# Decode attention beside a Mish block: keys loaded in 32 KB runs, scores made piece by piece, three value buffers for four

## The chip, the cores and the metric

One core of a Trainium2 chip runs the whole program. The time is the device time of one execution in microseconds; a kernel's time is the median over its runs. The profile shows one further execution instruction by instruction.

## The reference

One decode step of a transformer layer whose attention branch and dense branch stand side by side:

```python
xn = layernorm(x)                                   # x: 2 x 1 x 448
q = (xn @ wq) as 16 heads of 256                    # 8 key/value heads, 2 query heads on each
k, v = the last 4096 of 32768 cached rows per head  # 2 x 8 x 4096 x 256
p = softmax(q k^T / 16)
attn = (p v, heads joined) @ wo                     # 4096 x 448
h = xn @ w1 + b1                                    # 448 x 1792
dense = (h * tanh(softplus(h))) @ w2                # 1792 x 448
out = x + attn + dense
```

All inputs are bfloat16. The windows of the two caches are 33.55 MB each; the four weight matrices bring the traffic to 77.66 MB. There is one token per sequence, so each cached number is used for two query heads only.

## The kernel before, in words

**Units.** The 16 (batch, head) streams are worked on in U = 4 units of J = 4 streams. A unit has 8.39 MB of keys and 8.39 MB of values. Four key tiles (`load_k(u, r)`, r = 0 to 3) and four value tiles (`load_v(u, g)`, g = 0 to 3) of 2.097 MB bring them: 128 partitions of 16 KB, each a contiguous run in the cache. For keys, a partition is one of 32 chunks of 128 rows of one stream, so that its four tiles are four consecutive quarters of 64 KB. For values, a partition has 32 consecutive rows.

**Keys.** VectorE transposes each key tile in 32 x 32 blocks (`turn`, L267) into two buffers `kt[0]` and `kt[1]`: each of them holds one half of the rows of all four tiles, so a scores call needs the first or the second half of every tile of the unit. `scores(u, i)` (L329) adds a mask with one matmul, then makes the scores with 32 matmuls on four column groups of TensorE; ScalarE takes the exponential (L351), and VectorE transposes it to the probabilities `p_t[i]` (L357). `weigh(u)` sums them.

**Values.** `values(u, g)` (L389) multiplies with 16 matmuls into one PSUM tile. `gather` copies that tile and folds it, `finish` divides by the sum, `relay` and `mix_early` apply the output projection of a unit as soon as its weight `wo` is there. `carry` moves what they have gathered to the accumulator of the last unit, whose last value tile has a form of its own (`values_fixed`) and whose projection (`mix`) is followed by the down projection of the dense branch (`dense_out`), in the order of the four pieces in which its weight arrives (`load_w2`).

**Order.** The schedule is written out by hand: each engine runs its instructions in the order in which the program has them. All large loads stand in SyncE's queue. A load into a buffer whose earlier contents are still being read waits in that queue, and what stands behind it waits too. Buffers per partition: three key tiles of 16 KB (`k_pool`), and a ring of four value tiles of 16 KB (`v_pool`) that also takes the query projection's weight in two pieces and the up projection's.

In each unit the loads stand in the order: four values of this unit, three keys of the next, the output weight, the fourth key. The scores of a unit come after all four of its key tiles have been transposed, and before its values.

Of the kernel before, what the change touches and what calls it, by code (L numbers as in the profile page):

```python
# [17 lines left out]
def kernel(  # L18
# [13 lines left out]
    nc = tc.nc  # L32
    P = 128
    G = 4
    J = 4
    R = 4

    Bsz, Sq, D = A_x.shape
    _, Hkv, Sk, Dh = A_k_cache.shape
# [24 lines left out]

    ctx.enter_context(tc.manual_schedule())

    k_pool = ctx.enter_context(tc.tile_pool(name="kk", bufs=3))
    v_pool = ctx.enter_context(tc.tile_pool(name="vv", bufs=4))
    kt_pool = ctx.enter_context(tc.tile_pool(name="kt", bufs=1))
    wo_pool = ctx.enter_context(tc.tile_pool(name="wo", bufs=2))  # L70
    p_pool = ctx.enter_context(tc.tile_pool(name="pp", bufs=1))
# [17 lines left out]
    k_t, v_t, wo_t = {}, {}, {}  # L89

    def load_k(u, r):
        t = k_pool.tile([P, KE], BF16, tag="k", name="k")
        src = kview[u][:, s0:, :].rearrange("j (c t) d -> c j (t d)", c=C)
        nc.sync.dma_start(out=t[:], in_=src[:, :, r * KE : (r + 1) * KE])  # L94
        k_t[u, r] = t

    def load_v(u, g, lo=0, hi=T):
        if lo == 0:
            v_t[u, g] = ring("v")
        t = v_t[u, g]  # L100
        src = vview[u][:, s0:, :].rearrange("j (g x t) d -> g x j (t d)", g=G, x=C)
        nc.sync.dma_start(
            out=t[:, lo * Dh : hi * Dh], in_=src[g, :, :, lo * Dh : hi * Dh]
        )

    def load_wo(u):
        w = wo_pool.tile([P, KU, rep, 2 * D], BF16, tag="wo", name="wo")
        if u < U - 1:
            nc.sync.dma_start(
                out=w[:].rearrange("p k h e -> p (k h e)"),  # L110
                in_=A_wo.rearrange("(k u y i) d -> u y k (i d)", k=KU, u=U, i=8)[u],
            )
        for k2 in range(KU if u == U - 1 else 0):
            r0 = (u + U * k2) * rep * Dh
            nc.sync.dma_start(  # L115
                out=w[:, k2, :, :],
                in_=A_wo[r0 : r0 + rep * Dh, :].rearrange("(h p c) d -> p h (c d)", h=rep, p=P),
            )
        wo_t[u] = w
# [4 lines left out]
    nc.scalar.dma_start(out=b1_sb[:], in_=B_b1.rearrange("(k q c) -> q k c", k=2, q=P))  # L124

    load_k(0, 0)
    load_k(0, 1)
    wq_t = []
    wq_in = A_wq.flatten().rearrange("(p e) -> p e", p=P)
    for lo, hi in ((0, 4), (4, NS)):  # L130
        t = ring("wq")
        nc.sync.dma_start(out=t[:, 0 : (hi - lo) * HW], in_=wq_in[:, lo * HW : hi * HW])
        wq_t += [t[:, i * HW : (i + 1) * HW] for i in range(hi - lo)]
    load_k(0, 2)

    ident = consts.tile([P, P], BF16)
    make_identity(nc, ident[:])
# [65 lines left out]
    for s in range(NS):  # L203
        r = s // 2
        step = 3 + s % 2
        if s % 4 == 0:
            xrows = small.tile([P, 4, P // 2, 2], BF16, tag="ex", name="xrows")
        xrow = xrows[0:Bsz, s % 4, :, :]
        nc.vector.tensor_copy(out=xrow, in_=xn_v[:, :, r : r + step + 1 : step])  # L209
        nc.tensor.transpose(  # L210
            xr_ps[:, s, :], xrow.rearrange("b a o -> b (a o)"), ident[0:Bsz, 0:Bsz]
        )
# [32 lines left out]
    def add_rows(lhsT, rows, stop=False):  # L245
# [8 lines left out]
            )  # L254

    kt = [
        kt_pool.tile([P, TH * NB, P // (R * J), R, J], FP32, name=f"kt{i}") for i in range(NH)
    ]
    ktm = [
        kt[i][:].bitcast(BF16).rearrange("p (t n) c r (j e) -> p n e t (c r j)", n=NB, e=2)  # L260
        for i in range(NH)
    ]

    def turn(u, r, i):
        t = k_t[u, r]
        w = TH * Dh
        nc.vector.transpose(  # L267
            out=kt[i][:, :, :, r, :],
            in_=t[:, i * w : (i + 1) * w].bitcast(FP32).rearrange(
                "p (a c j) -> p a c j", c=P // (R * J), j=J  # L270
            ),
        )

    spread = {}
    for n in range(2):
# [9 lines left out]
    def project():  # L285
        q_ps = ps_m.tile([P, 512], FP32, tag="m", name="q_ps")
        for s in range(NS):
            for u in range(U):
                nc.tensor.matmul(  # L289
                    q_ps[32 * u : 32 * (u + 1), :],  # L290
                    lhsT=xs[:, s, :],
                    rhs=wq_t[s][:, u * 512 : (u + 1) * 512],
                    start=(s == 0),
                    stop=(s == NS - 1),
                    skip_group_check=True,
                )
        q_sb = consts.tile([P, 4, P], BF16)
        nc.scalar.copy(out=q_sb[:].rearrange("p a m -> p (a m)"), in_=q_ps[:])
        qt_ps = ps_m.tile([P, 4, P], BF16, tag="m", name="qt_ps")
        for a in range(4):  # L300
            nc.tensor.transpose(qt_ps[:, a, :], q_sb[:, a, :], ident[:])  # L301
        qT = consts.tile([P, 2, U, Bsz, KU, rep], BF16)
        q_v = qt_ps[:].rearrange("p (h c) (u r) -> p c u r h", c=2, u=U)
        for c in range(2):
            for b in range(Bsz):
                nc.vector.tensor_copy(  # L306
                    out=qT[:, c, :, b, :, :], in_=q_v[:, c, :, b : KU * Bsz : Bsz, :]
                )
        qr_ps = ps_m.tile([P, 2 * NB, U, NQ], FP32, tag="m", name="qr_ps")
        for n in range(NB):  # L310
            for e in range(2):
                nc.tensor.matmul(
                    qr_ps[:, 2 * n + e, :, :].rearrange("p u q -> p (u q)"),
                    lhsT=spread[n % 2, e][:].rearrange("p g a -> p (g a)"),
                    rhs=qT[:, n // 2].rearrange("p u b k h -> p (u b k h)"),
                    start=True,
                    stop=True,
                    skip_group_check=True,
                )
        for g in range(G):  # L320
            rows = slice(g * 32, (g + 1) * 32)
            nc.vector.tensor_copy(
                out=qd[rows, :, :, g, :],
                in_=qr_ps[rows].rearrange("p n u q -> p u n q"),
            )
# [1 line left out]
    p_t = [p_pool.tile([P, G, TH, NQ], BF16, name=f"p{i}") for i in range(NH)]  # L327

    def scores(u, i):  # L329
        sc = ps_sc.tile([P, TH, 32], FP32, tag="sc", name="sc")  # L330
        nc.tensor.matmul(  # L331
            sc[:].rearrange("p t m -> p (t m)"),
            lhsT=ident[:],
            rhs=mneg[:].rearrange("p a j -> p (a j)"),
            start=True,
            stop=False,
            skip_group_check=True,
        )
        for n in range(NB):
            for e in range(2):  # L340
                for w in range(4):
                    nc.tensor.matmul(  # L342
                        sc[32 * w : 32 * (w + 1), :, :],
                        lhsT=qd[:, u, 2 * n + e, :, :].rearrange("p g q -> p (g q)"),
                        rhs=ktm[i][:, n, e, :, 32 * w : 32 * (w + 1)],
                        start=False,
                        stop=(n == NB - 1 and e == 1),
                        skip_group_check=True,
                    )
        ex = small.tile([P, TH, 32], BF16, tag="ex", name="ex")  # L350
        nc.scalar.activation(  # L351
            out=ex[:].rearrange("p t m -> p (t m)"),
            in_=sc[:].rearrange("p t m -> p (t m)"),
            func=ACT.Exp,
            scale=scale,
        )
        nc.vector.transpose(  # L357
            out=p_t[i][:].rearrange("p g t q -> p t g q"),
            in_=ex[:].rearrange("p t (g q) -> p t g q", g=G),
        )  # L360

    state = {}

# [172 lines left out]

    def load_w2(part):
        if part == 0:
            state["w2"] = k_pool.tile([P, KE], BF16, tag="k", name="w2")
        k, lo, hi = w2_parts[part]  # L540
        w2_in = B_w2.flatten().rearrange("(k p e) -> k p e", k=2, p=P)
        at = k * NI * D
        nc.sync.dma_start(
            out=state["w2"][:, at + lo * D : at + hi * D],
            in_=w2_in[k, :, lo * D : hi * D],
        )
# [6 lines left out]
                act_bf[:, i, k, :], state["w2"][:, at : at + D], stop=(k == 1 and i == NI - 1)  # L553
            )

    def turns(u, r):
        for i in range(NH):
            turn(u, r, i)

    load_w1()  # L560
    load_k(0, 3)
    turns(0, 0)
    turns(0, 1)
    project()
    turns(0, 2)
    dense_in()
    turns(0, 3)
    mish()
    for u in range(U):
        last = u == U - 1  # L570
        if last:
            load_wo(u)
        load_v(u, 0)
        load_v(u, 1)
        load_v(u, 2)
        if last:
            load_v(u, 3, 0, 24)
            load_v(u, 3, 24, T)
            for part in range(len(w2_parts)):
                load_w2(part)  # L580
        else:
            load_v(u, 3)
            load_k(u + 1, 0)
            load_k(u + 1, 1)
            load_k(u + 1, 2)
            load_wo(u)
            load_k(u + 1, 3)
        if u > 0:
            relay(u - 1)
            mix_early(u - 1)  # L590
        if last:
            carry()
        scores(u, 0)
        scores(u, 1)
        weigh(u)
        for g in range(G - 1):
            values(u, g)
        if not last:
            values(u, G - 1)
            turns(u + 1, 0)  # L600
            turns(u + 1, 1)
            gather(u)
            finish(u)
            turns(u + 1, 2)
            turns(u + 1, 3)
    u = U - 1
    gather(u, last=False)
    values_fixed(u, G - 1, 0, 24)
# [45 lines left out]
```

The softmax here doesn't subtract the row's maximum and nothing guards it: scores larger than these inputs give would overflow.

## Time and profile before

| | |
|---|---|
| median of 3 runs | 192.1 us (191.95 to 192.65) |
| span of the profiled run | 190.1 us |
| DMA | 77.66 MB on the main queue, 409 GB/s over the span |
| TensorE (PE) busy | 79.8 us, 42% |
| VectorE (DVE) busy | 91.5 us, 48%, of which 72.1 us key transposes |
| ScalarE busy | 12.3 us, 6% |
| chain that ended last | DMA 85%, DVE 10%, issue 3% |

The profile cuts the span into 40 slices of 4.75 us and gives each engine's busy share in tenths, and the bytes moved by the core's 16 DMA engines as GB/s. In its groups of instructions, "out<-in" has the names of the program's tiles, and L267 is line 267 of the program. In the timeline a row gives start, duration, engine, line and what the engine had waited for. The windows give each engine's busy time in a stretch, then the clock granted to TensorE (1.00 is full), the DMA share and the rate.

### The profile page before, as it was taken

The page shows a single profiled execution, that of the slowest core. Times are in us where ns is not written, and L with a number is a line of the kernel's source. Part 1 is how long each engine was busy: PE and PEld are TensorE (multiplying, and loading weights), DVE is VectorE, ACT ScalarE, POOL GpSimd, SP SyncE. Part 2 cuts the span into 40 slices and gives each one's busy share as a digit, 9 for nine tenths or more (in the row PEclk, how much of TensorE's full clock was granted, in tenths as well). Part 3 has the DMA queues.
Part 4 walks back from the last instruction along what each step waited for, and adds up shares of the span by engine and source line. Part 5 has one row for each costly group of instructions (what it writes and reads, how often), then busy time and mean ns, then how long its engine had stood idle before and what let it go on. Part 6 is the DMA issues. An engine that isn't in the chain of part 4 may idle for free.

```text
span 190.1 us, 2021 instructions
## 1 busy us (share of the span) xinstructions
PE 79.8 (42%) x873; PEld 37.8 (20%) x873; DVE 91.5 (48%) x97; ACT 12.3 (6%) x23; POOL 4.0 (2%) x16
## 2 busy tenths in 40 slices
PE   0301525197316016296233017394252026575384
PEld 0100115032104012032014012131022021221182
DVE  6887067583001999553003996823006994831001
ACT  3000030011001000011001000020010001020001
POOL 8000000000000000000000000000000000000000
PEclk9999999999965555869955555889755557696555
DMA  6999999999999999999999999999999999999990
GB/s 221 390 435 427 442 418 434 424 422 428 428 431 428 421 427 425 431 434 424 424 428 428 434 421 428 428 431 421 438 424 421 422 433 400 434 428 418 416 377 29
DMA packets 7025, 77.79 MB, mean 409 GB/s; under 512 B 997, under 2 KB 1769, under 8 KB 2537
## 3 DMA queue, kind: packets, MB, share of 16 engines
q1 hardware_dynamic: 6740, 77.66, 96.8%
q8 instruction: 6, 0.10, 0.2%
q10 hardware_dynamic: 276, 0.01, 0.1%
q14 instruction: 3, 0.02, 0.0%
HBM read 77.67 MB, written 0.00 MB: 409 GB/s over the span
## 4 chain that ended last, share of the span: by engine, by line
DMA 85%; DVE 10%; issue 3%; SPq 1%; PE 0%; DVEq 0%
DMA k<-in_A_k_cache_dram 66%; DMA w<-in_B_w_dram 12%; DVE kt L267 10%; DMA wo<-in_A_wo_dram 7%; PE acc L247 0%; SPq L115 0%; SPq L94 0%; DVEq L649 0%; DVE res L620 0%; DVE oT L436 0%
## 5 line engine op out<-in xcount | busy, mean ns | idle before, releaser
L267 DVE STREAM_TRANSPOSE kt<-k 128x2048 f32<-128x2048 f32 x32 | 72.1, 2290 | 55.5 <-DMA k<-in_A_k_cache_dram 55.4
L389 PE MATMUL pv<-v,p 128*32 128x512 bf16 x240 | 19.4, 462 | 25.7 <-DMA v<-in_A_v_cache_dram 25.7
L342 PE MATMUL sc<-kt,qd 128*32 128x512 bf16 x256 | 22.0, 500 | 13.9 <-DVE kt L267 13.9
L389 PEld LDWEIGHTS <-p 128*32 128x32 bf16 x240 | 7.0, 107 | 41.3 <-issue 37.8
L452 PE MATMUL ox_ps<-oT,hot 128*64 128x4 bf16 x48 | 2.3, 192 | 29.7 <-DVE oT L436 29.7
L342 PEld LDWEIGHTS <-qd 128*32 128x32 bf16 x256 | 8.5, 115 | 25.5 <-issue 23.1
L357 DVE STREAM_TRANSPOSE p<-ex 128x512 bf16<-128x512 bf16 x8 | 5.7, 712 | 13.1 <-ACT ex L351 13.1
L471 PE MATMUL early<-wo,ox 128*2 128x448 bf16 x24 | 9.4, 571 | 5.1 <-DMA wo<-in_A_wo_dram 5.1
L409 PE MATMUL o<-sel,vs 128*128 128x8 f32 x32 | 7.5, 363 | 2.9 <-ACT vs L403 2.9
L409 PEld LDWEIGHTS o<-sel,vs 128*128 128x128 f32 x32 | 7.1, 325 | 6.5 <-ACT vs L403 6.5
L289 PE MATMUL q_ps<-wq,xs 128*32 128x512 bf16 x28 | 3.4, 624 | 12.0 <-DMA wq<-in_A_wq_dram 12.0
L452 PEld LDWEIGHTS <-hot 128*64 128x64 bf16 x48 | 2.5, 151 | 29.6 <-issue 29.5
L351 ACT ACTIVATE ex<-sc 128x512 bf16<-128x512 f32 x8 | 4.8, 597 | 39.6 <-PE sc L342 39.6
L436 DVE TENSOR_TENSOR oT<-o,rec 128x16 bf16<-128x16 f32 x4 | 0.6, 145 | 12.7 <-PE o L424 12.7
L403 ACT COPY vs<-pv 128x512 f32<-128x512 f32 x4 | 2.3, 586 | 49.8 <-PE pv L389 49.8
L367 PE MATMUL dn<-p,ones 128*128 128x512 bf16 x8 | 3.1, 383 | 4.5 <-DVE p L357 4.5
L501 PE MATMUL h_ps<-xs,w 128*128 128x4 bf16 x49 | 2.8, 193 | 4.9 <-DMA w<-in_B_w_dram 4.9
L471 PEld LDWEIGHTS <-ox 128*2 128x2 bf16 x24 | 2.8, 115 | 9.6 <-issue 8.5
L331 PE MATMUL sc<-mneg,ident 128*128 128x512 bf16 x8 | 4.1, 514 | 0.0
L210 PE MATMUL xr_ps<-ident,xrows 2*128 2x2 bf16 x7 | 1.0, 180 | 6.6 <-DVE xrows L209 6.6
L289 PEld LDWEIGHTS <-xs 128*32 128x32 bf16 x28 | 1.0, 126 | 13.9 <-issue 13.9
L306 DVE COPY qT<-qt_ps 128x16 bf16<-128x16 bf16 x4 | 0.4, 167 | 6.9 <-PE qt_ps L301 6.9
(62 smaller groups left out, 39.9 us busy)
## 6 DMA issues: line engine op xcount, KB each, us to landing
k<-in_A_k_cache_dram SPq DMA_DIRECT2D x16, 2048.0 KB, 18.0
v<-in_A_v_cache_dram SPq DMA_DIRECT2D x15, 2048.0 KB, 25.1
wo<-in_A_wo_dram SPq DMA_DIRECT2D x3, 896.0 KB, 31.4
wq<-in_A_wq_dram SPq DMA_DIRECT2D x1, 2048.0 KB, 16.2
w<-in_B_w_dram SPq DMA_DIRECT2D x1, 1568.0 KB
wq<-in_A_wq_dram SPq DMA_DIRECT2D x1, 1536.0 KB, 19.3
v<-in_A_v_cache_dram SPq DMA_DIRECT2D x1, 1536.0 KB, 27.8
wo<-in_A_wo_dram SPq DMA_DIRECT2D x2, 448.0 KB, 13.2
```

The source lines that it names most:

```text
L267: nc.vector.transpose(out=kt[i][:, :, :, r, :], in_=t[:, i * w : (i + 1) * w].bitcast(FP32).rearrange("p (a c j) -> p a c j", c=P // (R * ...
L289: nc.tensor.matmul(q_ps[32 * u : 32 * (u + 1), :], lhsT=xs[:, s, :], rhs=wq_t[s][:, u * 512 : (u + 1) * 512], start=(s == 0), stop=(s == N ...
L331: nc.tensor.matmul(sc[:].rearrange("p t m -> p (t m)"), lhsT=ident[:], rhs=mneg[:].rearrange("p a j -> p (a j)"), start=True, stop=False, ...
L342: nc.tensor.matmul(sc[32 * w : 32 * (w + 1), :, :], lhsT=qd[:, u, 2 * n + e, :, :].rearrange("p g q -> p (g q)"), rhs=ktm[i][:, n, e, :, 3 ...
L351: nc.scalar.activation(out=ex[:].rearrange("p t m -> p (t m)"), in_=sc[:].rearrange("p t m -> p (t m)"), func=ACT.Exp, scale=scale,)
L357: nc.vector.transpose(out=p_t[i][:].rearrange("p g t q -> p t g q"), in_=ex[:].rearrange("p t (g q) -> p t g q", g=G),)
L367: nc.tensor.matmul(dn[:].rearrange("p a q -> p (a q)"), lhsT=ones[:], rhs=p_t[i][:].rearrange("p g t q -> p (g t q)"), start=(i == 0), sto ...
L389: nc.tensor.matmul(pv[32 * w : 32 * (w + 1), :, :].rearrange("p x d -> p (x d)"), lhsT=p_t[a // 4][:, g, 4 * (a % 4) : 4 * (a % 4) + 4, :] ...
L409: nc.tensor.matmul(po[:, c, :], lhsT=sb[:, x, c::2], rhs=sel[:, x, :], start=(x == 0 and c == 0), stop=(last and x == 1), skip_group_check ...
L452: nc.tensor.matmul(ox_ps[rows, y, :, :], lhsT=hot[:, k, y, :, :].rearrange("p q k -> p (q k)"), rhs=oT[:, :, k * rep + h, :], start=(y == ...
L471: nc.tensor.matmul(early[:], lhsT=ox[:, i, :], rhs=w[:, i, :], start=False, stop=(u == U - 2 and i == 7),)
L501: nc.tensor.matmul(h_ps[:, i, :, :].rearrange("p k b -> p (k b)"), lhsT=w1_v[:, s, i, :], rhs=xs[:, s, 0 : 2 * Bsz], start=(s == 0), stop= ...
```

## The change

A unit's keys come in two tiles of 4.19 MB instead of four of 2.097 MB, with 32 KB in one run per partition. With the tile's two quarters transposed into one `kt` buffer, a scores call needs one key tile instead of half of all four, so the first scores of the next unit are made while its second key tile is under way. The loads of a unit are put in a new order: the first keys of the next unit, two values, the second keys, two values, the output weight. The key pool goes from 3 x 16 KB to 2 x 32 KB, the ring of values from four tiles to three, so that the sum per partition stays the same. The purpose is fewer and longer runs for the keys, and work on keys and values that is spread over the unit.

```diff
-    k_pool = ctx.enter_context(tc.tile_pool(name="kk", bufs=3))
-    v_pool = ctx.enter_context(tc.tile_pool(name="vv", bufs=4))
+    k_pool = ctx.enter_context(tc.tile_pool(name="kk", bufs=2))
+    v_pool = ctx.enter_context(tc.tile_pool(name="vv", bufs=3))
...
     def load_k(u, r):
-        t = k_pool.tile([P, KE], BF16, tag="k", name="k")
+        t = k_pool.tile([P, RK * KE], BF16, tag="k", name="k")
         src = kview[u][:, s0:, :].rearrange("j (c t) d -> c j (t d)", c=C)
-        nc.sync.dma_start(out=t[:], in_=src[:, :, r * KE : (r + 1) * KE])
+        nc.sync.dma_start(out=t[:], in_=src[:, :, r * RK * KE : (r + 1) * RK * KE])
...
     kt = [
-        kt_pool.tile([P, TH * NB, P // (R * J), R, J], FP32, name=f"kt{i}") for i in range(NH)
+        kt_pool.tile([P, T * NB, P // (R * J), RK, J], FP32, name=f"kt{i}") for i in range(NH)
     ]
...
+    def turns(u, i):
+        t = k_t.pop((u, i))
+        for r in range(RK):
+            nc.vector.transpose(
+                out=kt[i][:, :, :, r, :],
...
                     nc.tensor.matmul(
-                        sc[32 * w : 32 * (w + 1), :, :],
+                        sc[32 * w : 32 * (w + 1)].rearrange("p t c m -> p t (c m)"),
                         lhsT=qd[:, u, 2 * n + e, :, :].rearrange("p g q -> p (g q)"),
-                        rhs=ktm[i][:, n, e, :, 32 * w : 32 * (w + 1)],
+                        rhs=ktm[i][:, n, e, :, 16 * w : 16 * (w + 1)],
...
+        nc.scalar.activation(out=ex[:, :, :, i, :], in_=sc[:], func=ACT.Exp, scale=scale)
+        if i == NH - 1:
+            for h in range(NH):
+                nc.vector.transpose(
+                    out=p_t[h][:].rearrange("p g t q -> p t g q"),
...
+    turns(0, 0)
+    project()
+    scores(0, 0)
+    turns(0, 1)
+    dense_in()
+    mish()
+    scores(0, 1)
+    weigh(0)
+    for u in range(U - 1):
+        load_k(u + 1, 0)
+        load_v(u, 0)
+        load_v(u, 1)
+        load_k(u + 1, 1)
+        load_v(u, 2)
+        load_v(u, 3)
+        load_wo(u)
+        turns(u + 1, 0)
+        values(u, 0)
+        values(u, 1)
+        scores(u + 1, 0)
+        turns(u + 1, 1)
+        values(u, 2)
+        values(u, 3)
+        gather(u)
+        finish(u)
+        scores(u + 1, 1)
+        weigh(u + 1)
+        relay(u)
+        mix_early(u)
+    u = U - 1
+    load_v(u, 0)
+    load_v(u, 1)
+    load_wo(u)
+    load_v(u, 2)
+    load_v(u, 3, 0, 24)
+    load_v(u, 3, 24, T)
+    for part in range(len(w2_parts)):
+        load_w2(part)
+    carry()
+    for g in range(G - 1):
+        values(u, g)
```

What follows in the last unit (its gathering, the last value tile, the projections and the result's store) is as before. In the names of the prediction, K0 and K1 are the two key tiles of a unit, V0 to V3 its value tiles.

## The prediction

> **What bounds the kernel now.** I read four views in this order: the slices with the DMA rate, the chain that ended last, the windows by stretch, and the timeline at a few handovers.
>
> ```profile
> DVE  6887067583001999553003996823006994831001
> ...
> DMA  6999999999999999999999999999999999999990
> GB/s 221 390 435 427 442 418 434 424 422 428 428 431 428 421 427 425 431 434 424 424 428 428 434 421 428 428 431 421 438 424 421 422 433 400 434 428 418 416 377 29
> ...
> q1 hardware_dynamic: 6740, 77.66, 96.8%
> ...
> DMA k<-in_A_k_cache_dram 66%; DMA w<-in_B_w_dram 12%; DVE kt L267 10%; DMA wo<-in_A_wo_dram 7%; PE acc L247 0%; SPq L115 0%; SPq L94 0%; DVEq L649 0%; DVE res L620 0%; DVE oT L436 0%
> ```
>
> The DMA row is full from the second slice to the last but one, while VectorE has empty slices in every unit. 85% of the chain is transfers. The 10% that the chain puts on the key transpose (L267) is not lost time: the DMA row shows no hole there. So the time is bytes divided by rate, plus start and end, unless a wait empties the queue. The windows give the rate:
>
> ```profile
> 2.00:5.00 3.00, 0.00 (x0) 0.00 (x0) 2.47 (x10) 1.31 (x2) 2.55 (x10) 1.00 0.98 361
> ...
> 15.00:175.00 160.00, 69.95 (x689) 31.12 (x690) 78.78 (x63) 9.67 (x18) 0.00 (x0) 0.74 1.01 427
> ```
> ```profile
> 36.00:55.00 19.00, 10.21 (x115) 3.56 (x115) 7.63 (x12) 1.42 (x3) 0.00 (x0) 0.96 1.01 428
> ...
> 97.00:107.00 10.00, 3.77 (x24) 2.40 (x24) 4.20 (x2) 0.59 (x1) 0.00 (x0) 0.50 1.00 426
> ```
> ```profile
> 184.00:184.50 0.50, 0.43 (x17) 0.34 (x13) 0.03 (x1) 0.00 (x0) 0.00 (x0) 0.50 1.14 425
> 184.50:185.00 0.50, 0.30 (x16) 0.30 (x20) 0.14 (x1) 0.00 (x0) 0.00 (x0) 0.50 0.70 264
> 185.00:185.20 0.20, 0.20 (x20) 0.20 (x12) 0.00 (x0) 0.00 (x0) 0.00 (x0) 0.50 0.33 134
> ...
> 186.20:186.70 0.50, 0.49 (x20) 0.31 (x16) 0.00 (x0) 0.00 (x0) 0.00 (x0) 0.50 0.11 36
> ```
>
> The last two columns are DMA share and GB/s: 427 steadily, 428 in a stretch of values, 426 in one of keys. From 184.5 us the rate falls while data still moves until about 186.6: the 16 engines don't finish together, the slowest is some 2 us behind the first.
>
> The timeline shows what a transfer costs, and the queue's reserve:
>
> ```profile
> 56.41 1.90 PE L389 MATMUL pv<-v,p 128*32 128x512 bf16 x16 [3.85 <-DMA v<-in_A_v_cache_dram]
> ...
> 61.28 4.50 DVE L267 STREAM_TRANSPOSE kt<-k 128x2048 f32<-128x2048 f32 x2 [13.95 <-DMA k<-in_A_k_cache_dram]
> ...
> 65.82 0.54 SPq L94 DMA_DIRECT2D k<-in_A_k_cache_dram  x1
> 66.17 4.50 DVE L267 STREAM_TRANSPOSE kt<-k 128x2048 f32<-128x2048 f32 x2 [0.38 <-DMA k<-in_A_k_cache_dram]
> ...
> 71.06 4.50 DVE L267 STREAM_TRANSPOSE kt<-k 128x2048 f32<-128x2048 f32 x2 [0.33 <-DMA k<-in_A_k_cache_dram]
> ```
>
> Three keys land 4.89 us apart: 2.097 MB each, 429 GB/s. The fourth key's issue at 65.82 waited for a transpose (it ended at 65.78), but keys landing at 66.17 and 71.06 and an output weight landing at 73.27 were still queued: over 7 us of reserve, so no hole.
>
> **What the Trainium skill says.** (1) "DMA: Bandwidth & Descriptors", section "Where 436 GB/s comes from": 16 ports of 32 B at 850 MHz, 435.2 GB/s, is the most the DMA can bring into SBUF. The trace's 427 to 429 lies 1.5 to 2% below; only that remainder can be won. (2) Same page, "Why small descriptors are slow (HBM only)": each packet has a fixed cost of about 3 cycles, and 32 bytes of metadata travel with each operation. The trace agrees that something is fixed: at 435.2 a 2.097 MB transfer would take 4.819 us, it takes 4.89, and the 0.071 us over 8 packets of 16 KB per engine are 8.9 ns each, more than the 3 to 4 cycles (about 4.7 ns, an estimate from that page). (3) Same page, "Anatomy of one DMA": DMA engines don't wait on semaphores, the issuing sequencer does. So a load that waits for a buffer holds back every load behind it on SyncE; the issue at 65.82 shows such a wait. (4) "SBUF — State Buffer", "SBUF: two separate sides": compute ports and DMA ports don't contend. The trace agrees: 426 GB/s in 97 to 107 us with VectorE 4.2 us busy, and 426 in 133 to 143 us with it idle. Moving transposes to other hours therefore leaves the rate alone.
>
> **The change part by part.**
>
> *Keys in 32 KB runs.* The bytes are the same, 33.55 MB of keys. Key packets per engine fall from 16 x 8 = 128 to 8 x 8 = 64. 64 x 8.9 ns = 0.57 us saved on the path, whether the fixed cost sits in the packet or at the end of a transfer, since both halve. Bounds: the page's 4.7 ns gives 0.3 us; a key stream without any fixed cost would save 16 x 0.071 = 1.14 us; a loss that is proportional to bytes gives 0. I take 0.6.
>
> *Compute.* 32 key transposes of 2048 elements (2.29 us) become 16 of 4096, which I price at 4.5 us: 9.0 us per 4.19 MB tile, as before. Scores keep 256 matmuls of 512 columns, 8 exps of 512 elements and 8 probability transposes; only strides and their hour differ. I price this at nothing, as VectorE's 91.5 us and PE's 79.8 us hide behind some 184 us of transfers. Bound from the other side: were the new stride to slow the transposes by a third, a tile would take 12 us, but there are only two in a unit of 41 us.
>
> *Buffers and order.* Keys: 2 x 32 KB for 3 x 16; values 3 x 16 KB for 4 x 16. Each load now waits for an earlier reader. Counted in a unit from the landing of its next keys' first half (key transfer 9.72, value 4.89, output weight 2.2; period 41.2 us): K0 0, V0 4.9, V1 9.8, K1 19.5, V2 24.4, V3 29.3, weight 31.5, next K0 41.2. Next K0 needs the transposes of this one, done at 9.0, and its data may start at 31.5. Next V0 needs the values of V1 (11.7, start 41.2); V1 needs V2 (26.3, start 46.1); K1 needs the transposes done at 28.5 (start 51.0); V2 needs V3 (31.2, start 60.7); V3 needs its own unit's V0, 48.0 (start 65.6). The reserve is 17 us and more. At the start: K0 lands near 13 us, is turned by 22.4, and the next K0's data can't start before the up-projection weight has landed, near 35. No hole.
>
> *The tight place* is the last unit, where no keys stand between its values any more. Its V3 (SyncE: and all of the down-projection weight behind it) waits for the buffer of its V0, so for values(3, 0), which PE reaches only after scores, relay, early mix and carry. These are rows of it at that stage (start, duration):
>
> ```profile
> 153.76 0.78 PE L452 MATMUL ox_ps<-oT,hot 128*64 128x4 bf16 x16 [9.87 <-DVE oT L436]
> ...
> 156.24 3.14 PE L471 MATMUL early<-wo,ox 128*2 128x448 bf16 x8 [1.71 <-DMA wo<-in_A_wo_dram]
> ...
> 159.48 0.52 ACT L234 COPY e_sb<-early 2x448 f32<-2x448 f32 x1 [4.73 <-PE early L471]
> ...
> 166.95 1.98 PE L342 MATMUL sc<-kt,qd 128*32 128x512 bf16 x32
> ...
> 170.69 1.05 PE L389 MATMUL pv<-v,p 128*32 128x512 bf16 x16
> ```
>
> From the landing of V3 of unit 2 (time 0), by the rows of the trace before: values 1.9 and the copy to 2.6, gather to 4.5, mask and scores 0.4 + 2.9 (2.0 at full clock, 3.4 at the slow one) to 7.8, exp 0.65, two transposes of 0.71 to 9.9, sum 0.4, relay 0.8 and cast 0.2 to 11.4, early mix 3.1 (1.6 at full clock) to 14.5, carry 0.6 + 0.4 to 15.5, values(3, 0) 1.05 to 16.6. Fast and slow clock give 15 to 17.9. The first load of the program was issued at 0.73 and moved data at 2.15, so data 1.4 us later: 18.0 (16.4 to 19.3). Queued until then: weight 2.2, V0 and V1 4.89 each, weight 2.4, V2 4.89: 19.3 us. The slowest engine therefore drains at about 19.1, just later than 18.0: cost 0 for it. Engines that run 2 us ahead drain at 17.3 and wait 0.7, which the end doesn't see. Range of this cost: 0 to 2 us. I take 0.
>
> *End.* The last weights land behind the same values, then 0.7 us of matmuls, the result's cast and its store: unchanged.
>
> Sum: 192.1 - 0.6 + 0 = 191.5.
>
> **Rivals.**
> - *Larger gain, 190.6.* Keys at the full ceiling (-1.14) and a part of the 2 us of spread between engines goes too, say -0.4. For it: the spread is there at the end. Against: nothing ties the spread to the run length.
> - *No gain, 192.1.* The 2% are lost in proportion to bytes. For: keys and values have equal rates whatever their addresses. Against: 8.9 ns is the same order as the skill's fixed cost.
> - *Slower, 193.3.* The last unit's V3 waits: all engines idle for up to 2 us less the 0.6 gained and some that the spread hides: +1.2. For: a reserve of only 1.1 us by my count, and a slow clock (0.50 in that stretch before). Against: the spread of the engines covers it, and PE may run quicker.
>
> **How the numbers follow.** Small gain 0.48, larger gain 0.26, none 0.10, slower 0.16. The 0.5% bounds are 191.1 and 193.1. Faster: the larger gain and a tenth from the small one's lower edge, 0.36. Same: the rest of the small gain and no gain, 0.48. Slower 0.16. Range: 190.4 (the larger gain with a little more) to 193.0, which leaves out most of the slower case and the far edge of the larger.
>
> **What would show it.** Right: key packets of 32 KB, the rate between 15 and 175 us at 429 to 431, the chain nearly all DMA, no slice below 9 in the DMA row. Wrong: a drop in the DMA row some 9 us before the last landing, with SyncE's wait for PE's values before the last V3 load (tail case); a rate still 427 (no gain); transposes clearly above 9.0 us per tile, or a hole inside a unit, would break the pricing of compute or of the buffers.

## The result, and the profile after

The changed kernel takes 194.59 us (193.54 to 195.09 in four runs) against 192.15 us before: ratio 1.0112, 95% interval 1.0074 to 1.0151. It is slower, by 2.4 us. The page of the changed kernel, slices, main queue and chain:

```profile
DMA  6999998999999999999999999999999999997990
GB/s 219 437 386 434 492 437 360 452 420 420 423 440 437 427 425 417 443 434 423 447 440 396 413 424 480 423 393 430 478 430 393 416 432 435 401 415 294 311 412 15
...
q1 hardware_dynamic: 5588, 77.66, 96.0%
...
DMA v<-in_A_v_cache_dram 58%; DMA k<-in_A_k_cache_dram 15%; DMA w<-in_B_w_dram 5%; PE pv L390 5%; DVE kt L267 2%; PE sc L345 2%; PE early L472 1%; PE o L410 1%; DVE p L356 1%; SPq L103 1%; SPq L544 1%; SPq L132 1%; SPq L95 1%; ACT ex L353 0%; ACT vs L404 0%
```

The queue has 1152 packets less (5588 for 6740): the 2048 key runs of 16 KB are 1024 of 32 KB, and with eight loads fewer go 128 small completion packets. The DMA row shows 9 in every slice from 34 us on until the one that begins at 172.8 us, which has a 7; its rate and that of the slice after it, 294 and 311, are those of a queue that ran empty and filled again. (The 8 in the slice from 28.8 us is no hole: a packet is booked in full where it starts, so with packets of 32 KB single slices are uneven, and 28 to 36 us taken together average 430 GB/s.) TensorE's share of the chain, 0% before, is now 11%. In order of time (start, duration, what), the part of the chain that leads there reads:

```profile
158.34 1.92 PE pv L390 x16
...
160.92 1.87 PE o L410 x8
...
163.23 3.56 PE sc L345 x30
166.82 0.61 ACT ex L353
167.45 1.31 DVE p L356 x2
...
169.94 2.86 PE early L472 x8
...
174.00 1.86 PE pv L390 x9
175.88 0.54 SPq L103
```

This is the wait of the tight place, and the sign that the prediction had named for its slower case: unit 2's last values land at 158.34, values(3, 0) end at 175.86, and at 175.88 SyncE issues the last V3. The drop comes nearly 14 us before the last landing, not some 9. The windows of that moment (last two columns: DMA share, GB/s), in the changed kernel:

```profile
174.00:175.00 1.00, 1.00 (x13) 0.38 (x16) 0.00 (x0) 0.00 (x0) 0.00 (x0) 0.50 1.00 426
175.00:176.00 1.00, 1.00 (x12) 0.31 (x8) 0.00 (x0) 0.00 (x0) 0.00 (x0) 0.50 0.46 197
176.00:177.00 1.00, 1.00 (x16) 0.42 (x9) 0.00 (x0) 0.00 (x0) 0.00 (x0) 0.50 0.19 82
177.00:178.00 1.00, 0.79 (x16) 0.28 (x12) 0.00 (x0) 0.00 (x0) 0.00 (x0) 0.94 0.81 197
...
181.00:182.00 1.00, 0.00 (x0) 0.00 (x0) 0.00 (x0) 0.00 (x0) 0.00 (x0) 0.50 0.89 283
```

The rate falls at 175, when the first engines have nothing left, and is back at 431 only after 183. (For the reason given above, a window of 1 us can be off by some tens of GB/s; several in a row count.) The loss has two parts: three microseconds in which many of the 16 engines are idle, and five more at 283 to 381 GB/s although the DMA share is 0.87 to 1.08, so packets are under way but take longer.

The trace also holds every packet by itself. By these, ten engines finish V2 between 175.2 and 175.5 us and the other six between 176.6 and 177.1. The last V3 comes in two pieces, of 12 KB and 4 KB per partition. The packets of its first piece start from 177.2 us on and take 0.61 us each, where the same packets take 0.46 us in the kernel before.

### The profile page after: what moved, and what is told of

It is laid out like the page before. It is cut to its first block, busy times and chain, and to the rows that moved or that the text cites. A ratio compares the mean times of both kernels' runs of the same rounds, so it can differ in the third digit from the quotient of the medians.

```text
span 192.0 us, 1986 instructions
## 1 busy us (share of the span) xinstructions
PE 88.5 (46%) x870; PEld 37.1 (19%) x873; DVE 89.3 (47%) x81; ACT 12.3 (6%) x23; POOL 4.0 (2%) x16
## 3 DMA queue, kind: packets, MB, share of 16 engines
q1 hardware_dynamic: 5588, 77.66, 96.0%
## 4 chain that ended last, share of the span: by engine, by line
DMA 79%; PE 11%; DVE 3%; issue 3%; SPq 2%; ACT 1%; DVEq 0%; ACTq 0%
DMA v<-in_A_v_cache_dram 58%; DMA k<-in_A_k_cache_dram 15%; DMA w<-in_B_w_dram 5%; PE pv L390 5%; DVE kt L267 2%; PE sc L345 2%; PE early L472 1%; PE o L410 1%; DVE p L356 1%; SPq L103 1%; SPq L544 1%; SPq L132 1%; SPq L95 1%; ACT ex L353 0%; ACT vs L404 0%
## 5 line engine op out<-in xcount | busy, mean ns | idle before, releaser
L267 DVE STREAM_TRANSPOSE kt<-k 128x4096 f32<-128x4096 f32 x16 | 70.1, 4420 | 40.7 <-DMA k<-in_A_k_cache_dram 40.6
L390 PE MATMUL pv<-v,p 128*32 128x512 bf16 x240 | 27.3, 608 | 56.7 <-DMA v<-in_A_v_cache_dram 56.7
L345 PE MATMUL sc<-kt,qd 128*32 128x512 bf16 x256 | 26.4, 582 | 4.6 <-DVE kt L267 2.3
L390 PEld LDWEIGHTS <-p 128*32 128x32 bf16 x240 | 8.7, 128 | 73.7 <-issue 66.0
L437 DVE TENSOR_TENSOR oT<-o,rec 128x16 bf16<-128x16 f32 x4 | 0.7, 176 | 31.4 <-PE o L410 16.6
L472 PE MATMUL early<-wo,ox 128*2 128x448 bf16 x24 | 7.8, 491 | 0.8 <-ACT ox L462 0.8
L410 PE MATMUL o<-sel,vs 128*128 128x8 f32 x32 | 6.7, 339 | 2.8 <-ACT vs L404 2.8
L502 PEld LDWEIGHTS <-w 128*128 128x128 bf16 x49 | 2.7, 152 | 5.2 <-DMA w<-in_B_w_dram 5.2
L376 DVE TENSOR_REDUCE rec<-dn 128x8 f32<-128x512 f32 x4 | 2.8, 692 | 1.9 <-PE dn L368 1.9
L425 PE MATMUL o<-p,v 128*128 128x8 bf16 x64 | 1.9, 168 | 2.5 <-DMA v<-in_A_v_cache_dram 2.5
L334 PE MATMUL sc<-mneg,ident 128*128 128x512 bf16 x5 | 3.0, 591 | 0.0
```

The lines of the kernel that those rows point to most:

```text
L267: nc.vector.transpose(out=kt[i][:, :, :, r, :], in_=t[:, r * KE : (r + 1) * KE].bitcast(FP32).rearrange("p (a c j) -> p a c j", c=P // (R ...
L334: nc.tensor.matmul(sc[:].rearrange("p t c m -> p (t c m)"), lhsT=ident[:], rhs=mneg[:].rearrange("p a j -> p (a j)"), start=True, stop=Fal ...
L345: nc.tensor.matmul(sc[32 * w : 32 * (w + 1)].rearrange("p t c m -> p t (c m)"), lhsT=qd[:, u, 2 * n + e, :, :].rearrange("p g q -> p (g q) ...
L376: nc.vector.tensor_reduce(out=rec[:], in_=dn[:].rearrange("p a q -> p q a"), axis=AXIS.X, op=ALU.add)
L390: nc.tensor.matmul(pv[32 * w : 32 * (w + 1), :, :].rearrange("p x d -> p (x d)"), lhsT=p_t[a // 4][:, g, 4 * (a % 4) : 4 * (a % 4) + 4, :] ...
L410: nc.tensor.matmul(po[:, c, :], lhsT=sb[:, x, c::2], rhs=sel[:, x, :], start=(x == 0 and c == 0), stop=(last and x == 1), skip_group_check ...
```

## The experiments

**1. The last V3 in a key buffer.** A key buffer has been free since the transposes.

```diff
-            v_t[u, g] = ring("v")
+            if u == U - 1 and g == G - 1:
+                v_t[u, g] = k_pool.tile([P, RK * KE], BF16, tag="k", name="v3")[:, 0:KE]
+            else:
+                v_t[u, g] = ring("v")
```

> The changed kernel, with the last unit's fourth value tile in a key buffer that has been free since the transposes, so that its load no longer waits for values(3, 0). Theory A (the loss is that wait: the queue empties near 175 us and refills slowly): the hole of 175 to 182 us goes, all else stays, and the whole gain on the keys (0.08 us on each of 8 tiles) shows: 191.5 us, 0.3% under the kernel before. Rival B (the loss comes from the new order or from a slower TensorE clock, and the wait is a symptom): it stays at 193.5 us or more.

Measured: 191.67 us, ratio to the kernel before 0.9971 (0.9960 to 0.9982). Its windows at the same place:

```profile
175.00:176.00 1.00, 1.00 (x16) 0.38 (x12) 0.00 (x0) 0.00 (x0) 0.00 (x0) 0.50 0.90 381
176.00:177.00 1.00, 1.00 (x16) 0.40 (x12) 0.00 (x0) 0.00 (x0) 0.00 (x0) 0.50 1.07 451
```

TensorE does the same work at the same slow clock (0.50 up to 178 us), with V3's wait gone. Over 175 to 183 us this kernel moves 3292 KB and the changed one 2209: 1083 KB, or 2.5 us at 427 GB/s, where the two spans differ by 2.4 us (192.0 and 189.6). So this one wait is the whole loss; 1.8 us of it fall in the first three windows, 0.7 us in the slow refill after them. By single packets, those of V3's first piece take 0.46 us here for 0.61: eight on each engine, 1.1 us of the loss. A slower TensorE clock is not the cause: the run with a mean clock of 0.628 took 191.94 us, the changed kernel 194.99 at 0.625.

**2. The values ahead of the projection.** The same wait, shortened by another order on TensorE, with all buffers as they are.

```diff
-        relay(u)
-        mix_early(u)
+        if u < U - 2:
+            relay(u)
+            mix_early(u)
...
+    values(u, 0)
+    relay(u - 1)
+    mix_early(u - 1)
     carry()
-    for g in range(G - 1):
+    for g in range(1, G - 1):
         values(u, g)
```

> The changed kernel with all buffers as they are, but unit 2's relay, early mix and the carry behind values(3, 0) on TensorE instead of ahead of it, some 4.8 us of the chain from 169.1 to 173.9 us. Theory A: values(3, 0) ends near 171 us, the last V3 is issued 4.5 us before the queue is empty, no hole: 191.5 us, as with another buffer. Rival B (not the wait): 193.5 us or more. Rival C (what TensorE has to do at the end is the bound, in whatever order): slower than with another buffer by 1 us or more, since the same work is then pushed behind.

Measured: 191.79 us, ratio 0.9968 (0.9957 to 0.9979), as with the other buffer. The values of the profiled run, and when the next ones had to wait for data again:

```profile
169.28 1.05 PE L390 MATMUL pv<-v,p 128*32 128x512 bf16 x16
...
177.76 1.80 PE L390 MATMUL pv<-v,p 128*32 128x512 bf16 x16 [2.99 <-DMA v<-in_A_v_cache_dram]
```

values(3, 0) end at 170.3, so the last V3 is issued 4.6 us before 175, when the first engines ran dry in the changed kernel, and that's enough: the packets of V3's first piece take 0.46 us here too. The projection's work, pushed behind, costs nothing: TensorE still waits 3 us for V2.

**3. Three value buffers in the old order.** The kernel before, with nothing else changed.

```diff
-    v_pool = ctx.enter_context(tc.tile_pool(name="vv", bufs=4))
+    v_pool = ctx.enter_context(tc.tile_pool(name="vv", bufs=3))
```

> The kernel before with three value buffers instead of four, nothing else. Theory A (three buffers only hurt together with the new order, in which the projection stands ahead of the values): its last V3 is issued when values(3, 0) ends, 171.8 us, some 5 us before the queue is empty: 192.1 us, no change. Rival D (three buffers are too few in themselves): a hole at the last V3 and 193.5 us or more.

Measured: 194.19 us, ratio 1.0097 (1.0081 to 1.0112). My expectation was wrong. Rival D had the time right but not the place; its cause is tested in experiment 8. The drops of the rate are in the inner units, in unit 1 from 90 us and in unit 2 from 132 us. Two windows and, from the timeline, SyncE's issue of unit 1's V3:

```profile
91.00:92.00 1.00, 0.00 (x0) 0.00 (x0) 0.00 (x0) 0.00 (x0) 0.00 (x0) 1.00 0.91 311
...
132.00:133.00 1.00, 0.95 (x20) 0.33 (x13) 0.07 (x1) 0.00 (x0) 0.00 (x0) 1.00 0.66 279
```
```profile
89.21 0.54 SPq L102 DMA_DIRECT2D v<-in_A_v_cache_dram  x1
...
93.60 1.58 PE L389 MATMUL pv<-v,p 128*32 128x512 bf16 x16 [3.57 <-DMA v<-in_A_v_cache_dram]
```

V3 is issued at 89.21, yet V2, ahead of it in the queue, lands only at 93.60: the slowest engine was never without work, by 3 us after taking off the 1.4 us to the first byte, and the rate still dropped to 311. The first engine finished V2 at 90.65, just when V3's data was due, so hardly an engine stood idle. The packets that started in 90 to 92 us took 0.70 to 0.74 us, for 0.62 in the microseconds before. This is the first direct sign of what was wrong in my count: the packets of a load issued late took longer even where hardly an engine ran dry.

**4. The same kernel as in 1, with keys in 16 KB runs.**

```diff
-        nc.sync.dma_start(out=t[:], in_=src[:, :, r * RK * KE : (r + 1) * RK * KE])
+        for h in range(RK):
+            nc.sync.dma_start(out=t[:, h * KE : (h + 1) * KE],
+                in_=src[:, :, (r * RK + h) * KE : (r * RK + h + 1) * KE])
```

> The kernel of the first experiment (last V3 in a key buffer), with each key tile loaded by two transfers of 16 KB runs instead of one of 32 KB. Theory A (the run's fixed cost is what the change gains): each key tile takes 9.78 instead of 9.70 us, so 0.6 us more than the first experiment, 192.1 us. Rival E (the gain of the first experiment comes from the order): the same time as the first experiment, within 0.2 us.

Measured: 192.59 us, ratio 1.0012 (1.0004 to 1.0019), 0.9 us more than in 1. So the gain comes with the keys' runs, and the new order as such brings none; at 1.0012 it costs 0.2 to 0.3 us. The edit doubles both the packets and the loads of the keys. The pages give what the main queue's packets took, as a share of the span, for experiment 1 and for this run:

```profile
span 189.6 us, 1985 instructions
...
q1 hardware_dynamic: 5588, 77.66, 96.5%
```
```profile
span 190.7 us, 1993 instructions
...
q1 hardware_dynamic: 6740, 77.66, 96.5%
```

That is 183.0 and 184.0 us on each engine. The difference of 1.0 us is nearly all of what separates the two profiled runs (191.67 and 192.75 us). Between 40 and 173 us a packet of 16 KB takes 0.616 us on average and one of 32 KB 1.219 us, 0.012 us less than two of 16 KB, so most of the gain sits in the packets and not in the number of loads. The spacing of single landings is too uneven for this: for the second key tile of units 1, 2 and 3, this run differs from experiment 1 by -0.21, +0.29 and +0.07 us.

**5. A longer chain.** Four matmuls that feed nothing stand between the carry and values(3, 0).

```diff
     carry()
+    sc = ps_sc.tile([P, T, 2, RK * J], FP32, tag="sc", name="sc")
+    for i in range(4):
+        nc.tensor.matmul(
+            sc[:].rearrange("p t c m -> p (t c m)"),
+            lhsT=ident[:],
+            rhs=mneg[:].rearrange("p a j -> p (a j)"),
+            start=True,
+            stop=True,
...
```

> The changed kernel with four more matmuls of 128x512 on TensorE, into a tile that nothing reads, between the carry and values(3, 0): at the slow clock 0.59 us each, so the last V3 is issued some 2.4 us later (1.6 us at full clock). Theory A (the end follows that issue one for one once the queue is empty): 194.6 + 1.6 to 2.4, 196.6 us. Rival F (the hole costs what a restart of an empty queue costs, however long it was): 194.6 to 195.2 us.

Measured: 195.93 us (194.40 to 197.12), ratio 1.0159 (1.0092 to 1.0227). The runs scatter too much for the slope. In the profiled run of 196.88 us V3 was issued near 178.6 us, 2.7 us after that of the changed kernel's profiled run, which took 194.2 us: 2.7 us for 2.7 us, as theory A has it for a queue that is empty already. By single packets the last engine finished V2 at 177.2 and V3's first data came at 179.9, so all 16 stood idle for 2.7 us. Rival F doesn't fit that run, but it would about fit the two fastest (194.40 and 194.97), so the slope rests on one pair of runs.

**6. A shorter chain.** The carry alone moves behind values(3, 0).

```diff
-    carry()
-    for g in range(G - 1):
+    values(u, 0)
+    carry()
+    for g in range(1, G - 1):
```

> The changed kernel with the carry alone moved behind values(3, 0): the chain is 1.1 us shorter (0.52 us copy, 0.55 us matmuls and the handovers), the last V3 is issued near 174.8 us instead of 175.9 us. Theory A (one for one): 193.5 us. Theory G (what counts is when the first of the 16 engines runs dry, near 175 us, not when the slowest does, near 177 us: as the first data comes 1.4 us after the issue, a hole remains, and the slow refill with it): 193.3 to 194.0 us. My prediction's count (engines that are ahead may wait for nothing lost): 191.7 us.

Measured: 193.37 us (192.72 to 194.60), ratio 1.0053 (1.0030 to 1.0077), 1.7 us above experiment 1. In the profiled run (192.99 us) V3 was issued at 173.62, 2.3 us earlier than in the changed kernel's profiled run and not the 1.1 expected. First data was thus due at 175.0, just when the first engine runs dry. Its windows:

```profile
175.00:176.00 1.00, 0.00 (x0) 0.00 (x0) 0.00 (x0) 0.00 (x0) 0.00 (x0) 1.00 1.03 344
...
179.00:180.00 1.00, 0.65 (x4) 0.66 (x4) 0.00 (x0) 0.29 (x1) 0.00 (x0) 0.73 0.83 233
```

No window here is without data, the DMA share stays at 0.83 to 1.10, and still the rate is below 410 in six of them in a row, from 175 to 181 us. By single packets V3's first data starts at 175.16 and the first engine finishes V2 at 175.18: no hole at all. But the packets of V3's first piece take 0.58 us for 0.46, 1.0 us on each engine, most of the 1.3 us by which this profiled run is longer than that of experiment 1. This speaks against my count (191.7 us). Of theory G it supports the slow refill, and shows that this needs no hole: even a reserve that just reaches is too short.

**7. Loads from an idle queue.** Experiment 1 with six loads after its store, each waiting until VectorE has read from the one ahead.

```diff
+    for i, (src, n) in enumerate(((v_in[0], KE), (k_in, KE), (v_in[1], KE), (k_in, 2 * KE),
+                                  (v_in[2], 3 * KE // 4), (k_in, 3 * KE // 4))):
+        nc.sync.dma_start(out=probe[:, 0:n], in_=src[:, :, 0:n])
+        nc.vector.tensor_copy(out=seen[:, i : i + 1], in_=probe[:, 0:1])
```

> The kernel of the first experiment, and after its result is stored six loads, each from an idle queue: values of 16 KB runs, keys of 16 KB runs, values again, keys of 32 KB runs, values of 12 KB runs (the shape of the last V3's first piece), keys of 12 KB runs. The time is longer by these loads and is not compared; what counts is the time from issue to landing. At the steady 26.7 GB/s per engine and 1.4 us to the first byte: 6.3, 6.3, 6.3, 11.1, 5.1, 5.1 us. Theory H (engines that start in step slow each other on the value layout, where neighbouring partitions are 16 KB apart, and not on the key layout, 64 KB apart): values 25 to 30% slower than that, 7.5 us and 6.1 us, keys as computed. Rival I (the start of any load is slow): both slower alike. Rival J (the slow refill of the changed kernel had another cause): both as computed.

Issues and landings in the timeline (the time of a load runs from SyncE's row to the VectorE row after it):

```profile
195.66 0.54 SPq L629 DMA_DIRECT2D probe<-in_A_k_cache_dram  x1
203.00 0.16 DVE L630 COPY seen<-probe 128x1 bf16<-128x1 bf16 x1 [7.37 <-DMA probe<-in_A_k_cache_dram]
203.19 0.54 SPq L629 DMA_DIRECT2D probe<-in_A_v_cache_dram  x1
210.31 0.16 DVE L630 COPY seen<-probe 128x1 bf16<-128x1 bf16 x1 [7.15 <-DMA probe<-in_A_v_cache_dram]
```

The six took 7.47, 7.34, 7.12, 12.37, 6.53 and 6.60 us. That is 0.8 to 1.5 us above what I had computed for each, on keys and values alike, once per shape and layout except for two loads of 16 KB values: rival I. Theory H, the value layout, falls. My sum left out the time from the last packet's end to VectorE's row, 0.3 to 0.4 us in each of the six; the rest, 0.4 to 1.1 us, is the load's own. The changed kernel's V3 (first piece, 12 KB runs) landed 7.1 us after its issue, more than the 6.5 us of the same shape here. Here the packets are slow at the start alone (those of 12 KB values 0.63 us in the first microsecond, 0.46 in the last two, 0.52 on average), there through most of the piece. So a start from idle explains only part of the slow refill.

**8. Three value buffers in the old order, with a key tile ahead of V3.** The kernel of experiment 3 with one more edit.

```diff
-            load_v(u, 3)
             load_k(u + 1, 0)
+            load_v(u, 3)
```

> The old order with three value buffers, which took 194.2 us against my 192.1, with one change in SyncE's queue: in units 0 to 2 the next unit's first key tile stands ahead of the waiting V3 instead of behind it. Theory K (its loss is the same as in the changed kernel: V3 waits for values(u, 0) and the queue behind it is thin, with drops of the rate at 91 and 132 us): 4.9 us more of queued data cover the wait in those units; what the last unit loses stays (its V3 has no keys to stand behind): 192.5 to 193.3 us. Rival L (three buffers cost something else, in every unit): 194 us as before it.

Measured: 192.52 us, ratio 1.0007 (0.9998 to 1.0017), better than I expected. With 4.9 us more in the queue while V3 waits, three buffers cost nothing that the runs can show. The loss in experiment 3 was therefore the thin queue, not the ring's size, and the last unit, for which I had allowed up to 0.8 us, costs next to nothing there: its V3 was issued at 172.35, 3.3 us before the first engine finished V2, and the packets of its first piece took 0.46 us.

**9. Both cures.** Experiments 1 and 2 in one kernel.

> The changed kernel with both cures, the last V3 in a key buffer and the projection of unit 2 behind values(3, 0). Theory A (either cure keeps the queue full, and then bytes at the steady rate set the end): no gain over either one alone, 191.7 us. Rival C (TensorE's work at the end still costs something): up to 0.3 us less.

Measured: 191.67 us, ratio 0.9966 (0.9953 to 0.9979). Nothing beyond either alone. All three cured kernels beat both the kernel before and the changed one.

## Why the prediction was wrong

- *Keys in 32 KB runs, -0.6 us*: right in its sum, in part by luck. The kernel without the wait ends at 191.67 us, where I had put 191.5. The runs alone are worth 0.9 us (experiments 1 and 4), 0.012 us per pair of packets where I had 0.0089, and the new order takes 0.2 to 0.3 back, which I had put at nothing. My sign for the gain, 429 to 431 GB/s between 15 and 175 us, didn't come: it is 428 in experiment 1 and in the changed kernel. Nor did it follow from my own sum, as 0.6 us in 190 is 0.3%, and that lifts 427 to 428.
- *Compute*: right. 16 transposes at 4.42 us, 70.1 us together. One scores call waited 2.3 us for one of them, and no load did so at a cost. PE's busy time rose from 79.8 to 88.5 us, hidden.
- *Buffers inside a unit, no hole*: right. The DMA row has no hole before 173 us. In the new order the next unit's second keys stand between V1 and V2, so V3 never waits with a thin queue, as it does in experiment 3.
- *The tight place*: right about the wait, what it hangs on, and the times. Counted from the landing at 158.34, I had gather to 4.5, scores to 7.8, probabilities to 9.9, mix to 14.5, carry to 15.5, values to 16.6; measured 4.45, 8.5, 10.4, 14.5, 15.7, 17.5, inside my 15 to 17.9. V2 landed at 19.26, for which I had 19.3. (My count of when engines drain is uneven: 19.1 for the slowest, but 17.3 for those 2 us ahead, which belongs to 19.3.)
- *The step that failed* follows from them: "data 1.4 us later: 18.0", "just later than 18.0: cost 0 for it". There I priced a late load only by when its first byte comes, and took it to move at the full rate from then on; its slow packets, the main term, I had put at nothing. Measured, the packets of V3's first piece took 0.61 us instead of 0.46, which is 1.1 us on each engine. In experiment 6, where no engine ran dry and my count gives no loss, it was 1.0 us by the packets and 1.7 us by the medians. Besides, my reserve of 1.1 us was gone: V3's data came from 18.9 on, and the slowest engine had finished V2 at 18.8, so that the late engines waited up to some 0.5 us.
- *"Engines that run 2 us ahead drain at 17.3 and wait 0.7, which the end doesn't see"*: not refuted. In experiment 1 the engines finish V2 from 175.1 to 177.1 and V3's first piece from 178.8 to 180.8, so the leads last. In the changed kernel they start again in step and finish that piece from 182.0 to 182.6, the slowest 1.8 us later than there. The lead is lost, but the wait of the engines ahead isn't needed for the loss.
- *The sum*: 2.4 us between the profiled runs, 2.9 between the medians, where the case that I gave 0.16 had "up to 2 us less what the spread hides" and ended too low at 193.3. Some 1.8 of the 2.4 us are there when V3's first piece has come. The rest shows at the very end, where one engine finishes the last weights at 188.6 and the others by 187.7; I know no reason for it. Removing the wait in two independent ways removed the loss; shortening it left a part.
- *Not settled*: why the packets of a load that is issued late are slow, and what sets the spread of the engines. The scatter of the changed kernel's runs (193.5 to 195.1) fits a chain on TensorE whose clock varies, since the run with the highest mean clock (0.754) is the fastest; the eight runs of experiment 6 show no such order, so I leave this open.

## What to carry to other kernels

Where transfers set the time, look for the load whose buffer is freed last before the end, and count what is queued ahead of it up to the moment when the first DMA engine runs dry, with several microseconds in hand: here issues 4.6 and 3.3 us ahead of that moment (experiments 2 and 8) cost nothing that could be measured, and one 1.4 us ahead, whose data came just then, cost 1.7 us (experiment 6). What lies between wasn't tested by itself, and 3.3 us is no safe limit: the last V3 of experiment 3, issued 3.7 us ahead, still had slightly slow packets (0.49 us for 0.46). A buffer that another stage has finished with was one cure; an order that frees the buffer first, and leaves work that nobody waits for until later, was the other, with the same time. A gain of 0.6 us on the keys is real, and one such wait, at 2.9 us, loses it several times over.

## What the runs showed of the hardware

A 2.1 MB load into an idle queue took 7.1 to 7.5 us from issue to landing (experiment 7), 1.4 us of it before the first data, where loads in a full queue land 4.89 us apart; a 4.19 MB load took 12.4, where 9.7 is its share in a full queue. A load issued when little was left ahead of it had slow packets even where no engine ran dry: 0.58 us for 0.46 (experiment 6). The 16 engines ran 2 us apart and kept their leads while the queue was full; after the hole they finished the next load within 0.6 us of each other. Key runs of 32 KB instead of 16 KB, with half the loads, brought 0.4% of the kernel's time (0.9971 for 1.0012); a packet of 32 KB took 1.219 us, two of 16 KB 1.231.
